# u's normalisation, the modulation and two table loads moved forward within the generation of a convolution kernel, and six reads of u's spectra issued ahead

## Chip, core and metric

One NeuronCore of a Trainium2 chip. The time is device microseconds of one execution. TensorE is called PE, VectorE DVE, ScalarE ACT, GpSimd POOL and SyncE SP, as in the profile.

## What is computed

A layer on 2048 tokens of width 512. A vector c gives six modulation rows of 512. u is normalised, modulated and convolved per channel with a kernel K of 2048 taps that is generated from 128 complex poles; then comes a second modulated block of two mixers.

```python
mod = (_silu(c) @ w_mod).reshape(c.shape[0], 6, 1, -1)        # sa, ca, ga, sb, cb, gb
h = _layernorm(x, axis=-1) * (1 + ca) + sa
# inside _A_ref, on h:
P = jnp.exp(logdA[:, :, None] * l[None, None, :])
K = jnp.einsum("dn,dnl,dn->dl", Cc, P, dB).real
y = irfft(rfft(up, 2 * L) * rfft(Kp, 2 * L))[:L] + u * Dskip
x = x + ga * y
h = _layernorm(x, axis=-1) * (1 + cb) + sb
x = x + gb * _B_ref(h, ...)      # spatial shift mixer (w1, w2), then channel mixer (w3, w4)
```

(The transforms are shown shortened; the reference pads to 2L and uses rfft2.)

## The kernel before

It has three stages in one program. Each engine takes its instructions in the order in which the code issues them (`tc.manual_schedule`), so the order of the source is the order of five queues.

**Generation** (to about 207 us). A loop over k makes the kernel K in 32 chunks. For each chunk PE forms angles (`turns`, L440 to L455: nine pairs of matmuls into a PSUM bank pair `xx`, of which there are two), ACT takes their sine and cosine into a tile `tr` (three of them), DVE multiplies these with magnitudes (`products`, L466, L472 in every second chunk, L475, L476), and PE reduces the products in a burst of 64 small matmuls (`burst`, L498), whose PSUM bank ACT copies to KX after each second chunk. The turns of chunk k + 2 are issued in chunk k, ahead of chunk k's products. The magnitudes of the next four chunks come from `exps`: in chunks 1, 5, 9, ... 25 PE makes five more `xx` banks and ACT takes their exponentials, which needs another function table than the sine, so that a table is loaded ahead of them and another behind.

Other work is hung into the chunks by a list `side[k]`: what it holds is issued at the end of chunk k, and what it puts into `later` at the start of chunk k + 1. The 16 blocks of u are normalised there: `u_stats(i)` (DVE L142, L143, then two small POOL operations), two chunks later `u_norm(i)` (DVE L417, L418), and for each pair of blocks `u_dft` in the two chunks that follow (PE L426), whose results ACT copies to a tile `vs` in `later` and SP stores to the DRAM array VU (L434). `at(i)` gives block i's chunk. The quarters of u (`xu`, two buffers), the six weights of the modulation (`wm`, one buffer; `load_mod`, `mod_parts`, `mod_sum`), and the tables of the second transforms (`load_t2`, L533, into buffers of `xu`; `load_tu`, L537, into that of `wm`) are loaded by SP in the same list.

**Spectra** (to about 305 us). `k_first` (L626) makes eight rounds of K's first transform from KX; ACT copies half of each to VK0 and DVE half to VK1. VK0 lies on memory that generation used, among it that of the `vs` tiles. Then come 16 steps (jh, kc). Step n: PE makes K's spectrum (`spectrum_k`, L680), DVE multiplies it with u's (`multiply`, L690, L692), PE transforms the product of step n - 1 back (`back`, L702), ACT copies that to a tile `z` (two of them), POOL stores z to the DRAM array ZT (L706), PE makes u's spectrum of step n + 1 (`spectrum_u`, L650) from a block read from VU, and ACT copies it to `us`. ACT's order in a step is z, then us. The blocks are read by SP (`load_vu`, L640) into a ring of seven buffers `ld` of 512 KB. The same ring takes w1 (L750) and the blocks of ZT that the inverse reads (L721). The quarters of x (L724), FI and w2 are on SP's queue too. SP waits for nothing but a free buffer and the data's source, so it runs ahead of the loop that issues its loads.

**Mixers** (the rest), bound by PE.

Of the kernel before, what the change touches and what calls it, by code (L numbers as in the profile page):

```python
# [102 lines left out]
def dram(t, off, ap):  # L103
    return bass.AP(tensor=t.tensor, offset=t.offset + off, ap=ap)


def body(ctx, tc, A):
# [100 lines left out]
    def load_mod(n):  # L208
        wmt[n] = KX[:, n * 2048:n * 2048 + 2048].rearrange("p (a b) -> p a b", a=4) if n < 3 else \
            wml.tile([128, 4, 512], F32, name="wm")  # L210
        Y.dma_start(wmt[n].rearrange("p a b -> p (a b)"), A["wm"][MODS[n]])


    def mod_parts(n):
        w = wmt[n]
        m = psu.tile([128, 512], F32, name="pu")
        for i in range(4):
            T.matmul(m[32 * i:32 * i + 32], scb[:, i:i + 1].to_broadcast([128, 32]), w[:, i], start=True, stop=True,
                     skip_group_check=True)
        return lambda: act(w[:, 0], m)  # L220

    def mod_sum(n):
        k = MODS[n]
        m = psu.tile([128, 512], F32, name="pu")
        T.matmul(m, SP4, wmt.pop(n)[:, 0], start=True, stop=True)
        if k in (1, 4):
            return lambda: act(mods[k], m, AF.Identity, bias=1.0)
        return lambda: act(mods[k], m)
# [51 lines left out]
    with tc.manual_schedule():  # L280
# [88 lines left out]
        sg, mc, rc, at, at0 = la.bitcast(I32), tmp("mc"), tmp("rc"), tmp("at"), tmp("at0")  # L369
# [136 lines left out]
    side = {k: [] for k in range(40)}  # L506
    for k in range(8):
        w, i = ("w3", k) if k < 4 else ("w4", k - 4)
        n = A[w].shape[0] // 4
# [1 line left out]
    for k in range(2):  # L511
        side[28 + 3 * k].append(lambda i=k * 256: P.dma_start(WD["w2"][i:i + 256], A["w2"][i:i + 256]))
    for n in range(3, 6):
        k = 7 * n - 9
        side[k - 4].append(lambda n=n: load_mod(n))
        side[k].append(lambda n=n: later.append(mod_parts(n)))
        side[k + 1].append(lambda n=n: later.append(mod_sum(n)))
    at = lambda i: 1 + (i * 28) // 16
    for i in range(16):
        side[max(at(i) - 2, 0)].append(lambda i=i: u_stats(i))  # L520
        side[at(i)].append(lambda i=i: u_norm(i))
# [14 lines left out]
        TU.append(wml.tile([128, 32, 64], F32, name="wm"))  # L536
        Y.dma_start(TU[0], A["TU"].rearrange("p (a b) -> p a b", a=32))  # L537

    side[24].append(load_t2)
    side[29].append(load_tu)  # L540
    side[31].append(load_t2)

    def add_skip(h, g0, g1):
        V.tensor_add(Kq[:, h, g0:g1, 31], DS[:, h * 64 + g0:h * 64 + g1], Kq[:, h, g0:g1, 31])
# [74 lines left out]
    def k_first(r):  # L619
        bank = lambda n: psa.tile([128, 4, 2, 64], F32, name=n)  # L620
        ps = [bank("pk1"), kbank([128, 4, 2, 64]), bank("pz"), kbank([128, 4, 2, 64])]
        kv = KX.rearrange("p (g x) -> p g x", g=64)
        for gl in range(8):
            for j in range(2):
                rows = slice(64 * j, 64 * j + 64)
                T.matmul(ps[2 * j + gl // 4][:, gl % 4].rearrange("p j x -> p (j x)"), kv[rows, r * 8 + gl], FK[rows],  # L626
                         start=True, stop=True)
        for q in (0, 2, 1, 3):
            g0 = r * 8 + q % 2 * 4
            o, i = VK[q // 2][:, :, :, g0:g0 + 4], ps[q].rearrange("p g j x -> p x j g")  # L630
            if q // 2:
                V.tensor_copy(o, i)
            else:
                act(o, i)
# [3 lines left out]
    def load_vu(jh, kc):  # L638
        t = vus[jh, kc] = block()
        Y.dma_start(t, dram(VU, jh * 1048576 + kc * 8 * 16384, [[256, 128], [32768, 4], [1, 256]]))  # L640
# [17 lines left out]
    def flip(kc):  # L658
        t = t3s[kc] = c2.tile([128, 8, 64], F32, name="T3", bufs=3)
        for gh in range(2):  # L660
            r = slice(gh * 64, gh * 64 + 64)
            P.tensor_scalar(t[r], T2[kc // 4][r, kc % 4 * 4:kc % 4 * 4 + 8, 64 - gh * 64:128 - gh * 64], -1.0, None, op0=OP.mult)
# [54 lines left out]
    def load_inv(jh, k, i=None, q=Y):  # L717
        if (jh, k) not in zis:
            zis[jh, k] = block()
        a, n = (0, 4) if i is None else (2 * i, 2)  # L720
        q.dma_start(zis[jh, k][:, a:a + n], dram(ZT[jh], (k * 4 + a) * 32768, [[256, 128], [32768, n], [1, 256]]))  # L721

    def load_x(g):
        Y.dma_start(X2[:, g * 4:g * 4 + 4].rearrange("p b d -> p (b d)"), A["x"][g])  # L724
# [11 lines left out]
    def inverse_parts(jh, g, pl, name):  # L736
        return [inv_half(jh, g, i, pl, name) for i in range(2)]

    def inverse(jh, g):
        for f in inverse_parts(jh, g, psa, "pz"):  # L740
            f()
# [353 lines left out]

    steps = [(jh, kc) for jh in range(2) for kc in range(8)]
    with tc.manual_schedule():
        load_vu(*steps[0])
        flip(0)
        Y.dma_start(Gm, A["G"].rearrange("p (a b) -> p a b", a=2))  # L1100
        for r in range(8):
            k_first(r)
            if r == 3:
                load_vu(*steps[1])
            if r == 6:
                load_vu(*steps[2])
        us = spectrum_u(*steps[0])
        split = None
        for n, st in enumerate(steps):
            p = spectrum_k(*st)  # L1110
            multiply(*st, us, p)
            if n == 7:
                v0x.close()
                pw2 = ctx.enter_context(pool("pw2", side="right", reuse_waits="tile"))
                pw1 = ctx.enter_context(pool("pw1", side="right", reuse_waits="tile"))
                W2h, W2l, ldw2 = weights(pw2, WD["w2"], 512, 512, "w2", 4)
                W1h, W1l, ldw1 = weights(pw1, A["w1"], 512, 512, "w1", 4)
            if n > 0:
                back(*steps[n - 1])
            if n == 15:  # L1120
                i1 = inverse_parts(0, 1, psb, "pk2")
            if n < 15:
                us = spectrum_u(*steps[n + 1])
            if n + 3 < 16:
                load_vu(*steps[n + 3])
            if n % 2 == 0 and n < 14:
                flip(steps[n + 2][1])
            if n in (3, 4, 6, 8):
                load_x(n - 3 if n < 5 else n // 2 - 1)
            if n == 9:  # L1130
                Y.dma_start(FI, A["FI"].rearrange("p (a b c) -> p a b c", a=32, b=2))
            if split:
                split()
                split = None
            if n in (8, 9):
                split = ldw1(two, n % 2 * 2, 2)
            if n == 10:
                for k in (0, 3, 4, 7):
                    load_inv(0, k)
            if n == 12:  # L1140
                inverse(0, 0)
                w2s = [ldw2(None, 2 * i, 2) for i in range(2)]
                for b in range(4):
                    half_stat(b, 0)
            if n == 13:
                inverse(0, 3)
                for k in (1, 2, 5, 6):
                    load_inv(0, k)
            if n in (14, 15):
                w2s.pop()()  # L1150
# [105 lines left out]
        n = cm.tile([128, 2, 512], F32, name="h2")  # L1256
# [18 lines left out]
        r = transposed(n)  # L1275
        split_w(1)
        r = parts_of(r)
# [4 lines left out]
        for g in range(8):  # L1282
            r = chan(g, r)
# [18 lines left out]
```

## Time and profile before

| | us |
|---|---|
| three runs | 688.5, 689.38, 691.06 (median 689.38) |
| profiled execution | 691.26 |
| its span, first to last instruction | 689.5 |
| PE, DVE, ACT, POOL busy | 642.6, 498.0, 331.2, 124.8 |
| mean granted TensorE clock | 0.989 of full |
| waits of POOL for DVE's statistics of u | 140.2 in 15 |
| waits of ACT (z) for stores of ZT | 8.7 in 3 |

The waits of an engine with time to spare cost nothing: POOL has nothing else to do between two statistics. A timeline's row has the start, the duration, the engine, the line, the operation, what is written from what, and in brackets the idle time ahead of it and what ended it. ACT's rows all name L115, the helper through which it is called, so they are told apart by their tiles.

### The profile page before, as it was taken

The page shows a single profiled execution, that of the slowest core. Times are in us where ns is not written, and L with a number is a line of the kernel's source. Part 1 is how long each engine was busy: PE and PEld are TensorE (multiplying, and loading weights), DVE is VectorE, ACT ScalarE, POOL GpSimd, SP SyncE. Part 2 cuts the span into 40 slices and gives each one's busy share as a digit, 9 for nine tenths or more (in the row PEclk, how much of TensorE's full clock was granted, in tenths as well). Part 3 has the DMA queues.
Part 4 walks back from the last instruction along what each step waited for, and adds up shares of the span by engine and source line. Part 5 has one row for each costly group of instructions (what it writes and reads, how often), then busy time and mean ns, then how long its engine had stood idle before and what let it go on. Part 6 is the DMA issues. An engine that isn't in the chain of part 4 may idle for free.

```text
span 689.5 us, 16884 instructions
## 1 busy us (share of the span) xinstructions
PE 642.6 (93%) x7195; PEld 509.2 (74%) x7195; DVE 498.0 (72%) x795; ACT 331.2 (48%) x505; POOL 124.8 (18%) x236
## 2 busy tenths in 40 slices
PE   1899999999999998977998999999999999999996
PEld 0456655655569776634887889999899889898895
DVE  7899999999996887986987967464574536363522
ACT  3878988889875557432444623123131312222121
POOL 4011112112103355413741101001010000000000
PEclk9999999999999999998999999999999999999999
DMA  8603264643739997967387010020100201010001
GB/s 299 284 2 79 75 218 105 209 121 85 275 85 317 354 335 258 346 204 226 108 257 240 1 32 32 16 77 15 47 31 17 77 1 62 1 49 13 1 31 31
DMA packets 51091, 86.42 MB, mean 125 GB/s; under 512 B 4676, under 2 KB 39496, under 8 KB 48424
## 3 DMA queue, kind: packets, MB, share of 16 engines
q1 hardware_dynamic: 46712, 66.74, 30.1%
q0 software_dynamic: 3440, 17.57, 7.4%
q8 instruction: 56, 0.92, 0.6%
q10 hardware_dynamic: 864, 1.05, 0.5%
q14 instruction: 19, 0.16, 0.1%
HBM read 59.12 MB, written 32.90 MB: 133 GB/s over the span
## 4 chain that ended last, share of the span: by engine, by line
PE 70%; DVE 6%; DMA 5%; ACT 3%; POOL 2%; issue 1%; ACTq 0%; SPq 0%; DVEq 0%; POOLq 0%
PE pm L841 7%; PE pm L838 7%; PE pm L839 7%; PE xx L448 7%; PE pa L954 6%; PE pa L955 6%; PE pa L962 6%; PE kp L498 3%; DMA ZT<-z 3%; PE ph L893 2%; PE ph L895 2%; PE ph L892 2%; DMA ld<-ZT 2%; PE pu L426 2%; PE pT L803 2%; PE pk L626 2%
## 5 line engine op out<-in xcount | busy, mean ns | idle before, releaser
L115 ACT ACTIVATE gh<-pm 128x512 fp32r<-128x512 f32 (+1 forms) x48 | 26.9, 560 | 200.7 <-PE pm L841 200.7
L838 PE MATMUL pm<-nh,w3h 128*128 128x256 f32 (+1 forms) x352 | 86.6, 281 | 2.7 <-ACT nh L115 2.7
L839 PE MATMUL pm<-nh,w3l 128*128 128x256 f32 (+1 forms) x352 | 86.3, 280 | 0.1
L946 DVE TENSOR_TENSOR gl<-gf,gh 128x512 fp32r<-128x512 f32 (+1 forms) x48 | 30.8, 643 | 68.4 <-ACT gf L115 68.4
L954 PE MATMUL pa<-w4h,gh 128*128 128x512 f32 (+1 forms) x176 | 69.6, 395 | 0.0
L838 PEld LDWEIGHTS pm<-nh,w3h 128*128 128x128 f32 (+1 forms) x352 | 66.0, 187 | 4.4 <-ACT nh L115 2.9
L955 PE MATMUL pa<-w4l,gh 128*128 128x512 f32 (+1 forms) x176 | 68.9, 392 | 0.0
L839 PEld LDWEIGHTS pm<-nh,w3l 128*128 128x128 f32 (+1 forms) x352 | 65.9, 187 | 2.2 <-DVE w3l L756 0.5
L765 POOL TENSOR_TENSOR rs<-mv,eps_t 128x1 f32<-128x1 f32 (+1 forms) x39 | 11.0, 282 | 282.4 <-DVE mv L771 265.4
L841 PE MATMUL pm<-nl,w3h 128*128 128x256 f32 (+1 forms) x352 | 55.0, 278 | 0.0
L449 PE MATMUL xx<-MG,ON 64*128 64x512 f32 x160 | 48.1, 397 | 0.0
L962 PE MATMUL pa<-w4h,gl 128*128 128x512 f32 (+1 forms) x176 | 48.0, 390 | 0.0
L448 PE MATMUL xx<-MG,ON 64*128 64x512 f32 x160 | 48.0, 396 | 0.0
L841 PEld LDWEIGHTS pm<-nl,w3h 128*128 128x128 f32 (+1 forms) x352 | 47.0, 187 | 0.0
L898 DVE TENSOR_TENSOR h<-h,ph 128x512 f32<-128x512 f32 x16 | 11.0, 687 | 45.1 <-PE ph L895 45.1
L466 DVE SCALAR_TENSOR_TENSOR e<-tr,p 128x512 f32<-128x512 f32 x64 | 41.1, 684 | 1.5 <-ACT tr L115 1.5
L498 PEld LDWEIGHTS kp<-e,e 128*32 128x32 f32 x2048 | 30.1, 110 | 12.7 <-issue 7.6
L475 DVE TENSOR_TENSOR e<-tr,p 128x1024 f32<-128x1024 f32 x32 | 39.0, 1220 | 0.0
L476 DVE TENSOR_TENSOR e<-tr,m 128x1024 f32<-128x1024 f32 x32 | 39.0, 1219 | 0.0
L115 ACT ACTIVATE p<-xx 128x1024 f32<-128x1024 f32 (+1 forms) x40 | 37.5, 979 | 2.2 <-PE xx L252 1.0
L962 PEld LDWEIGHTS pa<-w4h,gl 128*128 128x128 f32 (+1 forms) x176 | 33.0, 188 | 7.3 <-DVE gl L946 0.2
L115 ACT ACTIVATE tr<-xx 128x1024 f32<-128x1024 f32 x32 | 33.0, 1030 | 9.6 <-PE xx L449 7.9
(236 smaller groups left out, 1731.6 us busy)
## 6 DMA issues: line engine op xcount, KB each, us to landing
VU<-vs SPq DMA_DIRECT2D x64, 128.0 KB, 3.7
ld<-VU SPq DMA_DIRECT2D x16, 512.0 KB, 7.4
ZT<-z POOLq DMA_DIRECT2D x30, 256.0 KB, 6.2
ld<-ZT SPq DMA_DIRECT2D x12, 512.0 KB
Dw<-in_w POOLq DMA_DIRECT2D x8, 688.0 KB, 4.7
xu<-in_u SPq DMA_DIRECT2D x4, 1024.0 KB, 8.0
KX<-in_x SPq DMA_DIRECT2D x4, 1024.0 KB, 8.0
GD<-go SPq DMA_DIRECT2D x16, 256.0 KB, 2.3
```

What stands on the lines that cost most here:

```text
L115: return S.activation(out, in_, f, bias=bias, scale=scale)
L448: T.matmul(x[:, :512], la, ma, start=(i == 0), stop=(i == len(ops) - 1))
L449: T.matmul(x[:, 512:], lb, mb, start=(i == 0), stop=(i == len(ops) - 1))
L466: V.scalar_tensor_tensor(e0[:, 1, a], tr[:, 1, 0], 1.0 - 2.0 * a, mg[:, a], op0=OP.mult, op1=OP.mult)
L475: V.tensor_mul(e0[:, 0], tr[:, 0, 0:1].to_broadcast([128, 2, 512]), mg)
L498: T.matmul(kp[32 * j:32 * j + 32, (k % 2) * 4 + g], e1[:, r, d], e0[:, r, :, d * 32:d * 32 + 32], start=(r == 0), stop=(r == 1), skip_grou ...
L838: T.matmul(p, wh[:, k, c], hi[k], start=(k == 0), stop=False)
L839: T.matmul(p, wl[:, k, c], hi[k], start=False, stop=False)
L841: T.matmul(p, wh[:, k, c], lo[k], start=False, stop=(k == 3))
L954: T.matmul(acc[i], gh[:m, e, s], W4h[:m, f], start=(f == 0), stop=False)
L955: T.matmul(acc[i], gh[:m, e, s], W4l[:m, f], start=False, stop=False)
L962: T.matmul(acc[i], gl[:m, e, s], W4h[:m, f], start=False, stop=(f == 10))
```

## The change

Six edits. The blocks of u are spread over 24 chunks instead of 28, so that `at(i)` runs to 23 instead of 27; the quarters of u that are loaded in the list move with it. The modulation's last three parts go from chunks 12, 19 and 26 to 10, 16 and 22. The tables T2, TU, T2 are loaded in chunks 21, 25 and 27 instead of 24, 29 and 31. Six reads of VU are issued ahead of the first rounds, where one was, and the others in the places that a table `ahead` gives. No operation is added or taken away.

```diff
     for n in range(3, 6):
-        k = 7 * n - 9
+        k = 6 * n - 8
         side[k - 4].append(lambda n=n: load_mod(n))
         side[k].append(lambda n=n: later.append(mod_parts(n)))
         side[k + 1].append(lambda n=n: later.append(mod_sum(n)))
-    at = lambda i: 1 + (i * 28) // 16
+    at = lambda i: 1 + (i * 24) // 16
...
-    side[24].append(load_t2)
-    side[29].append(load_tu)
-    side[31].append(load_t2)
+    side[21].append(load_t2)
+    side[25].append(load_tu)
+    side[27].append(load_t2)
...
     with tc.manual_schedule():
-        load_vu(*steps[0])
+        for i in range(6):
+            load_vu(*steps[i])
         flip(0)
         Y.dma_start(Gm, A["G"].rearrange("p (a b) -> p a b", a=2))
         for r in range(8):
             k_first(r)
-            if r == 3:
-                load_vu(*steps[1])
-            if r == 6:
-                load_vu(*steps[2])
         us = spectrum_u(*steps[0])
         split = None
+        ahead = {1: 6, 2: 7, 3: 8, 4: 9, 5: 10, 6: 11, 7: 12, 9: 13, 11: 15}
...
-            if n + 3 < 16:
-                load_vu(*steps[n + 3])
+            if n in ahead:
+                load_vu(*steps[ahead[n]])
...
                 for k in (0, 3, 4, 7):
                     load_inv(0, k)
+                load_vu(*steps[14])
```

The first place is DVE from the end of chunk 25 to the start of chunk 28. e0 and e1 are products, xu is a quarter of u, and p1 and WN are magnitudes and weights of the poles. Before:

```order
L476 TENSOR_TENSOR e1_2572<-tr_2395,m1_2485 128x1024
L417 SCALAR_TENSOR_TENSOR xu_1767<-xu_1767,lum_2451,modu_117 128x512
L418 SCALAR_TENSOR_TENSOR xu_1767<-xu_1767,lur_2454,modu_117 128x512
L142 BN_STATS lus_2639<-xu_1767 128x6
L143 BN_AGGR lum_2640<-lus_2639 128x2
L466 SCALAR_TENSOR_TENSOR e0_2677<-tr_2467,p0_2270 128x512 x2
```

and two chunks on, between chunks 27 and 28:

```order
L476 TENSOR_TENSOR e1_2747<-tr_2546,m1_2681 128x1024
L259 TENSOR_TENSOR p1_2560<-p1_2560,WN_116 128x64x4
L417 SCALAR_TENSOR_TENSOR xu_1767<-xu_1767,lum_2640,modu_117 128x512
L418 SCALAR_TENSOR_TENSOR xu_1767<-xu_1767,lur_2643,modu_117 128x512
L466 SCALAR_TENSOR_TENSOR e0_2814<-tr_2663,p0_2564 128x512 x2
```

The same stretch, chunks 25 to 28, in the changed kernel:

```order
L476 TENSOR_TENSOR e1_2618<-tr_2447,m1_2533 128x1024
L466 SCALAR_TENSOR_TENSOR e0_2716<-tr_2515,p0_2316 128x512 x2
L472 TENSOR_TENSOR m1_2720<-p1_2260 128x1024
L475 TENSOR_TENSOR e0_2716<-tr_2515,p0_2316 128x1024
L476 TENSOR_TENSOR e1_2717<-tr_2515,m1_2720 128x1024
L466 SCALAR_TENSOR_TENSOR e0_2779<-tr_2592,p0_2322 128x512 x2
L475 TENSOR_TENSOR e0_2779<-tr_2592,p0_2322 128x1024
L476 TENSOR_TENSOR e1_2780<-tr_2592,m1_2720 128x1024
L259 TENSOR_TENSOR p1_2606<-p1_2606,WN_116 128x64x4
L466 SCALAR_TENSOR_TENSOR e0_2844<-tr_2702,p0_2610 128x512 x2
```

u's two normalisations and one statistic have left; the products are as they were.

The second place is ACT in the changed kernel from the exponentials of chunk 25 (p0, p1) to the sine and cosine of chunk 28 (tr_2702).

```order
L115 ACTIVATE p0_2668<-xx_2665 128x1024
L115 ACTIVATE p1_2606<-xx_2671 128x768
L115 ACT_TABLE_LOAD
L115 ACTIVATE turn1_357<-hpi_70 128x1
L115 ACTIVATE KX_87<-kp_2537 128x8x64
L115 ACTIVATE vs_2686<-pu_2677 128x512
L115 ACTIVATE vs_2686<-pu_2678 128x512
L115 ACTIVATE tr_2702<-xx_2693 128x1024
L115 ACTIVATE tr_2702<-xx_2704,hpi_70 128x1024
```

Before, the same nine stand at this place, with the results of another pair of u's blocks in vs: nothing moved for ACT here.

The third place is SP's queue behind the last table, which is T2's second half (xu<-in_T2); ld<-VU are the reads of u's spectra, Gm a small table, KX<-in_x a quarter of x. Before:

```order
L533 DMA xu_3042<-in_T2 128x2048
L640 DMA ld_3079<-VU_60 128x4x256
L1100 DMA Gm_3058<-in_G 128x128
L640 DMA ld_3181<-VU_60 128x4x256
L640 DMA ld_3255<-VU_60 128x4x256
L640 DMA ld_3353<-VU_60 128x4x256
L640 DMA ld_3427<-VU_60 128x4x256
L640 DMA ld_3498<-VU_60 128x4x256
L640 DMA ld_3572<-VU_60 128x4x256
L724 DMA KX_87<-in_x 128x2048
L640 DMA ld_3644<-VU_60 128x4x256
L724 DMA KX_87<-in_x 128x2048
```

and in the changed kernel, from the sixth read on:

```order
L640 DMA ld_3089<-VU_60 128x4x256
L1101 DMA Gm_3058<-in_G 128x128
L640 DMA ld_3431<-VU_60 128x4x256
L640 DMA ld_3502<-VU_60 128x4x256
L640 DMA ld_3576<-VU_60 128x4x256
L724 DMA KX_87<-in_x 128x2048
L640 DMA ld_3648<-VU_60 128x4x256
L724 DMA KX_87<-in_x 128x2048
```

Gm moved behind the sixth read, and the first quarter of x from behind the seventh read to behind the ninth; the second quarter from behind the eighth to behind the tenth.

## The prediction

> **What bounds the kernel now.** I read the page first, then the table of stages, then each engine's timeline from 130 to 300 us.
>
> ```profile
> span 689.5 us, 16884 instructions
> ...
> DVE  7899999999996887986987967464574536363522
> ...
> DMA  8603264643739997967387010020100201010001
> ```
>
> A slice is 17.2 us. DVE is full to about 207 us, the generation of the convolution kernel; the DMA engines are full from there to about 260 us, where the spectra are multiplied; from 330 us on PE is full, and the change has no instruction there. The table of stages (PE, PEld, DVE, ACT, POOL busy, clock, DMA share, GB/s) says the same closer:
>
> ```profile
> 170.00:190.00 20.00, 19.52 (x361) 12.49 (x361) 19.74 (x26) 18.00 (x23) 4.45 (x7) 1.00 0.79 262
> 190.00:207.00 17.00, 17.00 (x354) 10.79 (x342) 16.79 (x20) 12.41 (x16) 0.00 (x0) 1.00 0.40 88
> ```
>
> PE looks as full as DVE, but a busy PE is not one at its peak. What decides is the idle time of DVE. Between 36 us and the end of generation its timeline has only these idle spells (in brackets):
>
> ```profile
> 124.51 1.29 DVE L466 SCALAR_TENSOR_TENSOR e<-tr,p 128x512 f32<-128x512 f32 x2 [0.22 <-ACT tr L115]
> ...
> 146.46 1.29 DVE L466 SCALAR_TENSOR_TENSOR e<-tr,p 128x512 f32<-128x512 f32 x2 [0.67 <-ACT tr L115]
> ...
> 190.67 1.29 DVE L466 SCALAR_TENSOR_TENSOR e<-tr,p 128x512 f32<-128x512 f32 x2 [0.21 <-ACT tr L115]
> ...
> 206.85 0.48 DVE L544 TENSOR_TENSOR KX<-DS,KX 128x64 f32<-128x64 f32 x2
> ```
>
> That is 0.22 + 0.67 + 0.21 = 1.1 us in 171. Generation takes as long as DVE's work, so moving that work within it gains at most 1.1 us. But all three spells stand three chunks behind a group of exponentials: ACT had not made the sine in time. ACT is the engine that is nearly late, and u's work on DVE is what covers it.
>
> **Term 1, the end of generation.** The change adds no work there; it moves 16 blocks of u forward, so that DVE's last piece for u is in chunk 23 instead of 27. Here is DVE in chunks 24 to 27 now:
>
> ```profile
> 174.61 1.29 DVE L466 SCALAR_TENSOR_TENSOR e<-tr,p 128x512 f32<-128x512 f32 x2
> ...
> 178.08 0.75 DVE L417 SCALAR_TENSOR_TENSOR xu<-xu,lum,modu 128x512 f32<-128x512 f32 x1
> ...
> 180.44 1.28 DVE L466 SCALAR_TENSOR_TENSOR e<-tr,p 128x512 f32<-128x512 f32 x2
> ...
> 185.04 1.29 DVE L466 SCALAR_TENSOR_TENSOR e<-tr,p 128x512 f32<-128x512 f32 x2
> ...
> 188.51 0.42 DVE L259 TENSOR_TENSOR p<-p,WN 128x256 f32<-128x256 f32 x1
> 188.85 0.75 DVE L417 SCALAR_TENSOR_TENSOR xu<-xu,lum,modu 128x512 f32<-128x512 f32 x1
> ```
>
> The rows of L466 open chunks 25, 26, 27, and that at 190.67 opens 28. The products of 25 take 178.08 - 174.61 = 3.47 us, of 26 185.04 - 180.44 = 4.60, of 27 188.51 - 185.04 = 3.47, L259 0.34: together 11.88. u's work between them takes 180.44 - 178.08 = 2.36 and 190.67 - 0.21 - 188.85 = 1.61, together 3.97, and goes. ACT and PE in the same stretch:
>
> ```profile
> 174.99 1.10 PE L498 MATMUL kp<-e,e 128*32 128x64 f32 x64
> ...
> 178.33 1.03 ACT L115 ACTIVATE tr<-xx 128x1024 f32<-128x1024 f32 x1
> ...
> 180.56 1.28 ACT L115 ACT_TABLE_LOAD   x1
> 181.86 4.90 ACT L115 ACTIVATE p<-xx 128x1024 f32<-128x1024 f32 x5
> 186.77 1.28 ACT L115 ACT_TABLE_LOAD   x1
> ...
> 188.65 1.07 ACT L115 ACTIVATE vs<-pu 128x512 f32<-128x512 f32 x2
> 189.60 1.04 ACT L115 ACTIVATE tr<-xx 128x1024 f32<-128x1024 f32 x1
> ```
>
> The matmuls of chunk 24 (L498) cannot begin before DVE ends that chunk at 174.61. Behind them in PE's order come u's transform, whose eviction ACT makes, and the turns of chunk 27. From 178.33 ACT is never idle until the sine of chunk 28 ends at 190.64: sines, table, five exponentials, table, eviction, sine. None of this goes: in the changed order the transforms of the last blocks stand behind chunks 24 and 25, just where those of the blocks before stood. So from the end of chunk 24 to the start of chunk 28's products this path takes 190.67 - 174.61 = 16.06 us, whatever DVE does, and DVE has 11.88 us left. It will wait **16.06 - 11.88 = 4.2 us** for a sine before chunk 28. The 3.97 us are not saved, since they now stand ahead of chunk 24. The three old spells go, as the earlier groups have as much of u's work behind them as before or more (chunks 17 to 19: two normalisations of about 1.6 and two statistics of about 0.8, against one and one): -1.1. Sum: **+3.1 us** at the end of generation.
>
> Bounds: if the path starts at PE's row, 174.99, and PE has no lag, the wait is 15.68 - 11.88 = 3.8; if the two modulation steps that move from chunks 26 and 27 to 22 and 23 leave PE 1.5 us late there, 5.7; if the old spells stay, 1.1 more; if ACT should run ahead and nothing waits, -1.1. So -1.1 to +5.7, and I take 3.1, since every piece of the path has its own row. Chunks 28 to 31 stay as they are: DVE is never idle there now, and PE and ACT only lose work.
>
> ```profile
> xu<-in_u SPq DMA_DIRECT2D x4, 1024.0 KB, 8.0
> ```
>
> What moves on the queues costs nothing. A quarter of u (8.0 us to land) is asked for four chunks, over 20 us, ahead of its first statistic, as the modulation's tiles are ahead of their matmuls; POOL's roots stay two chunks ahead of the normalisation that reads them; T2 and TU go three or four chunks earlier on SP, among VU's stores, where the DMA share is 0.40 to 0.79. If one of them came late, DVE would wait for it as long as it is late: a whole landing, 8 us, at the worst.
>
> [...]
>
> **Term 2, the step from generation to the spectra.**
>
> ```profile
> 204.72 2.57 SPq L434 DMA_DIRECT2D VU<-vs  x4
> 207.39 0.54 SPq L533 DMA_DIRECT2D xu<-in_T  x1
> 212.65 0.39 SPq L640 DMA_DIRECT2D ld<-VU  x1
> ...
> 220.00 1.67 SPq L724 DMA_DIRECT2D KX<-in_x  x1
> ...
> 212.79 2.56 ACT L115 ACTIVATE VK<-pk 128x512 f32<-128x512 f32 x5 [4.04 <-DMA xu<-in_T]
> ...
> 210.26 1.17 PE L626 MATMUL pk<-FK,KX 64*128 64x128 f32 x17
> ...
> 214.44 1.17 PE L626 MATMUL pk<-FK,KX 64*128 64x128 f32 x17
> ...
> 216.22 1.17 PE L626 MATMUL pk<-FK,KX 64*128 64x128 f32 x17
> ```
>
> ACT's first copy into VK0 waits 4.04 us. The trace names the load of T2; by place, VK0 lies where the eviction buffers vs lay, so it is the last stores of VU, issued up to 207.3. In the changed kernel they end four chunks sooner and the wait goes. But PE's rounds, 216.22 - 214.44 = 1.78 us each, lost only 214.44 - 210.26 - 2 x 1.78 = 0.6 us by it, since the PSUM banks covered the rest: **-0.6**. The 4.04 is not the prize. The first read of VU goes out when the last matmul of generation has freed its buffer, at about 209.3 plus the shift, 3.4 us sooner in its stage; its first reader (224.4) doesn't wait for it now, so that is worth nothing directly.
>
> **Term 3, the spectra.** Six reads ahead are not new: SP runs ahead of the loop, and seven reads are issued between 212.65 and 220.00 now, as many as there are buffers. New is that the first quarter of x (1 MB, L724) stands behind two more reads, of which each needs a buffer that step 0 or 1 must free. It leaves at about 228 instead of 220, and the four quarters each move to about where the next one is now. What waits in this stage:
>
> ```profile
> 245.29 0.69 DVE L690 TENSOR_TENSOR ma<-pk,us 128x512 f32<-128x512 f32 x1 [3.19 <-ACT us L115]
> ...
> 263.19 0.69 DVE L690 TENSOR_TENSOR ma<-pk,us 128x512 f32<-128x512 f32 x1 [2.69 <-ACT us L115]
> ...
> 261.09 1.09 ACT L115 ACTIVATE z<-pz 128x512 f32<-128x512 f32 x2 [4.34 <-DMA ZT<-z]
> ...
> 252.91 8.02 DMA ZT<-z
> ...
> 244.00:248.00 4.00, 4.00 (x76) 2.43 (x78) 2.71 (x5) 3.75 (x9) 2.11 (x4) 1.00 1.07 416
> ```
>
> DVE waits for us, which ACT makes behind z, which waits for a store of ZT two steps old, 8 us long among the reads (the row of the chain at 252.91). The stage is short of DMA, and no byte goes away that is issued in it after 220. One more megabyte now falls between 245 and 262, where the stores are: at 416 GB/s 2.5 us if all of it counts; nothing if it fits into the lulls. Below nothing: 3.19 + 2.69 = 5.9 gained if both waits go. The stores of steps 0 and 1 meet the same reads as before, one of them a quarter of x, so the first wait should stay; of the second, part moves a step or two earlier. I take **+0.7**, near the lower price, as the lulls are short.
>
> [...] The issue rows at 212.65 and 220.00 show the reads as early as their buffers allow already.
>
> **Sum.** 3.1 - 0.6 + 0.7 = +3.2 us. The profiled execution took 691.26 us (span 689.5 and 1.8 around it); it lay 1.9 above the median of the runs, 689.38. So 694.5 beside that execution, and **692.6** beside the median, which I put down. About 0.5%, 3.4 us, is what a measurement of this kernel can tell from no change, and the forecast lies just under it.
>
> **Rivals**, beside the median:
> 1. *DVE is not starved*: PE and ACT get ahead in chunks 20 to 24, so that the exponentials stand ready. For it: PE loses work behind chunk 25. Against: PE's matmuls of chunk 24 need DVE's products, and ACT has no gap. -1.1 - 0.6 + 0.7 = -1.0: 688.4. By this the change doesn't do what its words say for generation, and little else.
> 2. *The change does what the early reads are for*: stores of ZT meet fewer reads and both waits go, with the starved DVE: 3.1 - 0.6 - 5.9 = -3.4: 686.0; together with rival 1, 681.8. Against: the megabyte that comes later.
> 3. *Clearly slower*: x and FI push each other among the stores. It decides once the stores of step 2 land over a microsecond later than now; then the whole megabyte counts (2.5) and PE's lag at chunk 24 too (5.7 - 1.1 = 4.6): 4.6 - 0.6 + 2.5 = +6.5: 695.9.
>
> **How the numbers follow.** Forecast (+2 to +5) 0.55, a little more of it under the bound of 3.4 than over it; rival 1 0.17; rival 2 0.12; rival 3 0.16. Within 0.5%: 0.29 of the forecast, rival 1's 0.17 and 0.03 of rival 2, 0.49. Slower: 0.26 + 0.16 = 0.42. Faster: 0.09. The range reaches from above rival 2's value to a little over rival 3's, 687 to 696.5, and leaves out about 0.15.
>
> **What would show it.** Right: one idle spell of 4 us on DVE's timeline ahead of the first product of chunk 28, put down to ACT's sine, and no other over 0.3; the row of L544 at about 210; no wait of ACT's first VK copy; waits of DVE for us that still add up to about 6. Wrong: L544 at 206 (rival 1), one of the two waits for us gone (rival 2), a new one of over 1 us between 247 and 258 (rival 3). A wait for a normalised block, or for a table, would break the whole account: I price none.

## The result, and the profile after

| | median | runs | profiled execution (span) |
|---|---|---|---|
| before | 689.60 us | 688.50 to 691.06 (4) | 691.26 (689.5) |
| after | 700.51 us | 696.30 to 701.15 (4) | 701.15 (699.4) |

The change makes the kernel **slower: ratio 1.0149, 95% interval 1.0124 to 1.0174**. The forecast was 692.6, with a range to 696.5. The sign of its sum was right, its size was not, and the likeliest of its three outcomes, within 0.5%, was not the one that came.

First the span of the changed kernel, from its page, and the group of the products, from the table of groups by line (behind the bars: busy time, mean ns of one, then the idle time of DVE ahead of them and what ended it). Before, that idle time was `1.5 <-ACT tr L115 1.5`.

```profile
span 699.4 us, 16893 instructions
...
L466 DVE SCALAR_TENSOR_TENSOR e<-tr,p 128x512 f32<-128x512 f32 x64 | 41.1, 684 | 10.6 <-ACT tr L115 9.0 <-PE kp L498 1.6
```

The busy time, 41.1 us, is the same to the digit; only the waiting has grown. DVE's timeline from 36 us to the end of generation says where (in brackets the idle time and what ended it; these are all its idle spells there):

```profile
106.15 1.29 DVE L466 SCALAR_TENSOR_TENSOR e<-tr,p 128x512 f32<-128x512 f32 x2 [0.54 <-ACT tr L115]
112.10 1.29 DVE L466 SCALAR_TENSOR_TENSOR e<-tr,p 128x512 f32<-128x512 f32 x2 [0.43 <-ACT tr L115]
130.89 1.29 DVE L466 SCALAR_TENSOR_TENSOR e<-tr,p 128x512 f32<-128x512 f32 x2 [2.11 <-ACT tr L115]
154.45 1.29 DVE L466 SCALAR_TENSOR_TENSOR e<-tr,p 128x512 f32<-128x512 f32 x2 [0.74 <-ACT tr L115]
182.43 1.29 DVE L466 SCALAR_TENSOR_TENSOR e<-tr,p 128x512 f32<-128x512 f32 x2 [0.57 <-ACT tr L115]
186.77 1.29 DVE L466 SCALAR_TENSOR_TENSOR e<-tr,p 128x512 f32<-128x512 f32 x2 [0.78 <-ACT tr L115]
193.03 1.29 DVE L466 SCALAR_TENSOR_TENSOR e<-tr,p 128x512 f32<-128x512 f32 x2 [1.56 <-PE kp L498]
197.33 0.42 DVE L259 TENSOR_TENSOR p<-p,WN 128x256 f32<-128x256 f32 x1 [0.73 <-ACT p L115]
201.21 1.29 DVE L466 SCALAR_TENSOR_TENSOR e<-tr,p 128x512 f32<-128x512 f32 x2 [3.46 <-ACT tr L115]
217.39 0.48 DVE L544 TENSOR_TENSOR KX<-DS,KX 128x64 f32<-128x64 f32 x2
```

The first four stand ahead of chunks 12, 13, 16 and 20 and add up to 3.82 us. The last five stand ahead of chunks 25, 26 and 27, of the weighting at the end of 27 (L259), and of chunk 28: 7.10. Together 10.92, where there were 1.10. The end of generation (L544) moved from 206.85 to 217.39, by 10.54; the waits are 9.82 of it.

Two more rows close the account, the first matmul of the spectra (L650) and the first normalisation behind the inverse (L774):

```profile
234.30 1.09 PE L650 MATMUL pk<-ld,wm 64*64 64x256 f32 x16
328.27 1.36 DVE L774 SCALAR_TENSOR_TENSOR h<-KX,mv,modg 128x512 f32<-128x512 f32 x2
```

In the kernel before they are:

```profile
224.36 1.09 PE L650 MATMUL pk<-ld,wm 64*64 64x256 f32 x16
317.91 1.36 DVE L774 SCALAR_TENSOR_TENSOR h<-KX,mv,modg 128x512 f32<-128x512 f32 x2
```

L650 is 9.94 later, so the step from generation to the spectra gained 0.60. L774 is 10.36 later, so the spectra lost 0.42. The span is 9.9 longer, so the mixers gave back 0.46. In this pair of executions all of the loss is in generation.

One thing there was not in the forecast at all: TensorE's granted clock (the third column from the end in the table of stages, whose columns are as in the prediction).

```profile
93.00:104.00 11.00, 11.00 (x79) 5.82 (x69) 10.78 (x15) 7.64 (x11) 1.97 (x3) 0.53 0.20 66
```

In the kernel before, such a stretch is shorter:

```profile
97.00:101.00 4.00, 4.00 (x31) 2.75 (x35) 4.00 (x6) 3.60 (x6) 0.00 (x0) 0.57 0.58 232
```

Inside the first stretch, from 94 to 103 us, the clock is 0.50: half of full. A mean of 0.53 over 11 us is then 2 x 0.47 x 11 = 10.3 us at half clock; 0.57 over 4 us is 3.4. The waits ahead of chunks 12 to 20 come behind the one, the three old spells (124, 146, 191 us) behind the other.

### The profile page after: what moved, and what is told of

Same layout as the page of the kernel before. It is cut to its first block, busy times and chain, and to the rows that moved or that the text cites. A ratio compares the mean times of both kernels' runs of the same rounds, so it can differ in the third digit from the quotient of the medians.

```text
span 699.4 us, 16893 instructions
## 1 busy us (share of the span) xinstructions
PE 648.0 (93%) x7195; PEld 511.1 (73%) x7195; DVE 498.6 (71%) x795; ACT 332.4 (48%) x505; POOL 122.7 (18%) x236
## 4 chain that ended last, share of the span: by engine, by line
PE 53%; DVE 7%; DMA 6%; issue 2%; POOL 2%; ACT 1%; ACTq 0%; DVEq 0%; POOLq 0%
PE pm L841 7%; PE pm L839 7%; PE pm L838 7%; PE pa L962 6%; PE pa L954 6%; PE pa L955 6%; DMA ZT<-z 4%; PE ph L893 2%; PE ph L895 2%; PE ph L892 2%; PE pk L626 2%; DMA ld<-ZT 2%; PE pT L803 2%; PE pk L680 1%; PE pz L702 1%
## 5 line engine op out<-in xcount | busy, mean ns | idle before, releaser
L115 ACT ACTIVATE gh<-pm 128x512 fp32r<-128x512 f32 (+1 forms) x48 | 26.9, 560 | 200.6 <-PE pm L841 200.6
L466 DVE SCALAR_TENSOR_TENSOR e<-tr,p 128x512 f32<-128x512 f32 x64 | 41.1, 684 | 10.6 <-ACT tr L115 9.0
L115 ACT ACTIVATE p<-xx 128x1024 f32<-128x1024 f32 (+1 forms) x40 | 37.6, 980 | 5.1 <-PE xx L252 3.5
L680 PE MATMUL pk<-VK,xu 64*64 64x128 f32 x768 | 38.7, 272 | 0.1
```

What stands on the lines that cost most here:

```text
L115: return S.activation(out, in_, f, bias=bias, scale=scale)
L466: V.scalar_tensor_tensor(e0[:, 1, a], tr[:, 1, 0], 1.0 - 2.0 * a, mg[:, a], op0=OP.mult, op1=OP.mult)
L680: T.matmul(p[gh][kk * 64:kk * 64 + 64, i, ro], w, VK[jh][rows, ri * 32 + k1].rearrange("p j g -> p (j g)"), start=(ri == 0), stop=(ri == 1 ...
```

## Experiments

Two theories stood against each other. **Cover**: DVE waits because u's work no longer stands behind the last group of exponentials (chunk 25), and because PE is late there by its own work. **Clock**: the loss is the longer stretch at half clock. A third, that the reads cost the time, was kept as a check. The table has each kernel against the kernel before on the same chip, and from its one profiled execution the start of L544 and the sum of DVE's waits from 36 us to there.

| kernel | ratio to before (95%) | L544 | DVE's waits | L544 less waits |
|---|---|---|---|---|
| before | | 206.85 | 1.10 | 205.75 |
| the change | 1.0149 (1.0124 to 1.0174) | 217.39 | 10.92 | 206.47 |
| gen | 1.0156 (1.0103 to 1.0209) | 213.46 | 7.46 | 206.00 |
| reads | 1.0022 (1.0005 to 1.0038) | 205.41 | 0 | 205.41 |
| mod | 1.0148 (1.0125 to 1.0172) | 217.39 | 11.51 | 205.88 |
| uonly | 1.0146 (1.0121 to 1.0172) | 214.04 | 8.27 | 205.77 |
| tail | 1.0082 (1.0054 to 1.0109) | 210.12 | 4.42 | 205.70 |
| spread20 | 1.0172 (1.0148 to 1.0196) | 216.17 | 9.92 | 206.25 |
| modfree | 1.0052 (1.0031 to 1.0073) | 211.41 | 5.52 | 205.89 |
| nofill | 1.0272 (1.0248 to 1.0296) | 221.83 | 15.71 | 206.12 |
| mod26 | 1.0113 (1.0073 to 1.0152) | 211.03 | 5.22 | 205.81 |
| morefill | 1.0160 (1.0137 to 1.0184) | 215.49 | 9.52 | 205.97 |
| bfill | 1.0042 (1.0023 to 1.0060) | 208.10 | 2.26 | 205.84 |
| keep28 | 0.9973 (0.9955 to 0.9992) | 205.51 | 0 | 205.51 |

The last column is the first finding: in fourteen kernels it stays between 205.4 and 206.5. DVE's own work in generation is nearly the same in all of them, so its waits are what differs, and each wait can be priced by its row.

### The parts of the change alone

**gen** has the generation of the change (all three edits there) and the reads of before; its edit is the first two hunks of the diff.

> The edits of generation alone (u's blocks over 24 chunks, the modulation at 6n-8, the tables at 21, 25, 27); the reads of the spectra as before. Cover theory (DVE waits because u's work no longer stands where ACT's groups of exponentials need cover, and PE is late by the denser work): the end of generation (first row of L544) at 216 to 218 instead of 206.9, the whole time +9 to +11, so 699 to 701. Clock theory (the time goes by how long TensorE is held at half clock, about 10 us near 95 us in the profiled execution of the change against 3.5 before): only the 4 to 6 us of waits from chunk 24 on stay if the held stretch is 3 to 4 us here, so L544 at 211 to 213 and the whole at 693 to 696; 5 us more only if the held stretch is again about 10 us. Reads theory (the loss comes from the reads after all): within 2 us of before.

Measured: 700.09 us, as slow as the whole change. Its profiled execution was its fastest, 696.12. Its waits, from DVE's timeline:

```profile
150.52 1.29 DVE L466 SCALAR_TENSOR_TENSOR e<-tr,p 128x512 f32<-128x512 f32 x2 [0.37 <-ACT tr L115]
178.50 1.30 DVE L466 SCALAR_TENSOR_TENSOR e<-tr,p 128x512 f32<-128x512 f32 x2 [0.56 <-ACT tr L115]
182.85 1.29 DVE L466 SCALAR_TENSOR_TENSOR e<-tr,p 128x512 f32<-128x512 f32 x2 [0.78 <-ACT tr L115]
189.11 1.29 DVE L466 SCALAR_TENSOR_TENSOR e<-tr,p 128x512 f32<-128x512 f32 x2 [1.56 <-PE kp L498]
193.40 0.43 DVE L259 TENSOR_TENSOR p<-p,WN 128x256 f32<-128x256 f32 x1 [0.73 <-ACT p L115]
197.28 1.29 DVE L466 SCALAR_TENSOR_TENSOR e<-tr,p 128x512 f32<-128x512 f32 x2 [3.46 <-ACT tr L115]
```

The generation is the same program as in the change, instruction for instruction. The last five waits are the same to 0.01 us (7.09 against 7.10). Before chunk 25 there is 0.37 instead of 3.82, and this execution has no half clock near 95 us, only 3.4 us of it near 55 (and 3.4 more from 211 us on, at the very end). So the account has two parts: **about 7.1 us that the order makes, and a part that comes with half clock.** The other three runs of gen took 697.62, 702.57 and 703.79 at mean granted clocks of 0.986, 0.978 and 0.975, against 0.989 for the profiled one. Neither theory alone had this; the cover theory gave too much for the order, the clock theory too little.

**reads** is the kernel before with the other three hunks only.

> The six reads ahead alone, generation as before. Cover theory and clock theory alike: L544 at 206 to 208; ACT's first copy into VK0 still waits about 4 us for the last stores of VU; from step 0 to the inverse's first normalisation (L774) 0 to +1 us longer; the whole within 1 us of before. Reads theory: +3 or more.

Measured: 690.82, 0.22% slower, which both theories had. From 36 us on DVE has no wait in this generation, which is that of the kernel before, and TensorE no half clock in it: the three old spells, 1.1 us, come with the half clock near 97 us of the execution that was profiled. ACT's wait for the last stores stays, as forecast:

```profile
211.45 2.56 ACT L115 ACTIVATE VK<-pk 128x512 f32<-128x512 f32 x5 [4.14 <-DMA VU<-vs]
```

**mod** moves the modulation alone, **uonly** u's blocks alone (one line each, the rest as before).

```diff
-        k = 7 * n - 9
+        k = 6 * n - 8
```

> The modulation's steps alone at chunks 10, 16, 22 instead of 12, 19, 26; u's blocks, tables and reads as before. Cover theory: u's work still stands behind every group of exponentials, so DVE's waits grow by 0 to 1.5 us, at chunks 25 and 26 (PE late by the modulation in chunk 22) and perhaps at 16; L544 at 207 to 208.5. Clock theory: the same unless the held stretch near 95 us is longer than 3.5 us, then half of the excess on top.

```diff
-    at = lambda i: 1 + (i * 28) // 16
+    at = lambda i: 1 + (i * 24) // 16
```

> u's blocks alone over 24 chunks; modulation at chunks 12, 19, 26, tables and reads as before. Cover theory: a wait of 4 to 6 us ahead of chunks 27 and 28, more if the modulation's step at 26 and 27 adds to PE there, and 1 to 4 us elsewhere; L544 at 212 to 217, the whole +5 to +10. Clock theory: L544 at 211 to 212 with a held stretch of 3 to 4 us, and 5 more with one of 10 us. If the loss belongs to the modulation's move, L544 at 210 or below.

Measured: 699.59 and 699.51, each as slow as both together. For mod every theory was wrong, by 9 us. uonly came near the cover theory: L544 at 214.04 as expected, 0.67 + 0.73 + 3.46 = 4.86 us of waits at chunks 27 and 28, and the whole 0.5 us above its range. PE's timeline shows what was overlooked; here is uonly, whose wait of 3.12 us ahead of chunk 16 follows:

```profile
122.21 1.02 PE L225 MATMUL pu<-wm,sp 128*128 128x512 f32 x2
123.16 1.07 PE L426 MATMUL pu<-xu,FU 64*64 64x512 f32 x2
125.90 1.08 PE L426 MATMUL pu<-xu,FU 64*64 64x512 f32 x6 [1.67 <-ACT modg L115]
```

u's transform (L426) takes two PSUM banks of the pool `pu`, the sum of a modulation step (L225) one, and the pool has two. Where both fall in one chunk, PE stands here until ACT has evicted the sum (1.67 us in the last row); and in a chunk with exponentials ACT is busy with these (before, 4.90 us for five of them and 1.28 for each table, in the rows of the prediction). In uonly, whose generation is at full clock throughout, it is chunk 13. In mod it is chunk 17, where the wait is 1.67 again and DVE then waits 6.33 ahead of chunk 20 (155.27 us), with 3.4 us of half clock in between; two more such stretches stand near 54 and 123 us in that execution, so not all of mod's 11.51 us is the bank's. The sums of the change lie in chunks 11, 17 and 23 and its transforms in 3, 4, 6, 7, ... 24, 25: no sum meets one. (The first part of a step, L218, takes a bank too, in chunks 10, 16 and 22, and there it does meet one; what that did is told further down.) So the two edits need each other, and what one alone costs says little about the pair.

**modfree** tests that: the modulation earlier too, but with its sums in chunks 9, 16 and 23, which no transform of the kernel before uses.

```diff
-        k = 7 * n - 9
+        k = 7 * n - 13
```

> The kernel before with the modulation's steps at chunks 8, 15 and 22, so that the sum of a step (chunks 9, 16, 23) never falls into a chunk in which u's transform takes both of its PSUM banks; the modulation alone at 10, 16, 22 had sums at 11 and 17, where it does, and was 10.6 us slower. Bank theory (PE stands still until ACT, busy with a group of exponentials, evicts the sum): no wait of PE for modg, no wait of DVE over 1 us, L544 at 205 to 208, the whole within 3 us of before. Density theory (any modulation step earlier than 12, 19, 26 makes PE late): +6 or more, as it was with 10, 16, 22.

Measured: 693.17, 6.4 us better than mod, with no wait of PE for modg. That is as the bank theory has it, but the two profiled executions differ in the clock too (three stretches at half clock in mod's generation, none in modfree's), so how much of the 6.4 us is the bank's is not shown. And some loss stays: DVE waits 2.85 ahead of chunk 20 and 0.73 + 1.94 at chunk 28. The steps now stand at 15 and 22, ahead of the groups in chunks 17 and 25; before, they stood at 19 and 26, behind them.

### The cover

**tail** keeps the last four blocks of u where they were before.

```diff
-    at = lambda i: 1 + (i * 24) // 16
+    at = lambda i: 1 + (i * (24 if i < 12 else 28)) // 16
...
-    side[27].append(load_t2)
+    side[31].append(load_t2)
```

> The changed kernel, but the last four blocks of u are normalised at chunks 22, 23, 25 and 27 as before (their transforms follow, the second half of T2 is loaded at 31); the first twelve blocks, the modulation and the reads stay as changed. Cover theory (DVE waits because nothing of u is left behind the group of exponentials in chunk 25): DVE's waits ahead of chunks 25 to 28, 7.1 us in the changed kernel, fall to 0 to 1.5; L544 at 207 to 210, the whole 689 to 694. Clock theory (the loss is from stretches at half clock in the denser first 24 chunks): no more than 2 us better than the changed kernel, 698 to 701.

Measured: 695.02. DVE's waits:

```profile
150.04 1.29 DVE L466 SCALAR_TENSOR_TENSOR e<-tr,p 128x512 f32<-128x512 f32 x2 [2.98 <-ACT tr L115]
193.94 1.29 DVE L466 SCALAR_TENSOR_TENSOR e<-tr,p 128x512 f32<-128x512 f32 x2 [1.44 <-ACT tr L115]
```

The wait of 7.1 us ahead of chunks 25 to 28 falls to 1.44, as the cover theory has it. Not all of the 5.66 is cover: with no transform of u in chunks 21 and 22, PE's burst of chunk 24 also comes only 1.60 us behind DVE (178.25 and 176.65), where the change has 3.69. By that estimate about 3.6 are left for the cover, near the 3.97 us of DVE's work that stands there again. The whole is 1 us above its range, for a reason that is the theory's own: with twelve blocks early and four late, no block is normalised between chunks 17 and 22, and the group in chunk 17 has lost its cover. There a wait of 2.98 came up (chunk 20).

**spread20** packs u's blocks closer still.

```diff
-    at = lambda i: 1 + (i * 24) // 16
+    at = lambda i: 1 + (i * 20) // 16
```

> The changed kernel with u's blocks over 20 chunks instead of 24, everything else the same. Cover theory: the group of exponentials in chunk 21 loses its cover too, so a second wait of about 4 us stands ahead of chunk 24, beside the one of 3.5 to 4.2 ahead of chunk 28; L544 at 219 to 222, the whole 702 to 706. Clock theory, or a loss from the modulation's place: no new wait at chunk 24, the whole within 3 us of the changed kernel.

Measured: 701.62, L544 3 us earlier than expected, but with the second wait just where the cover theory puts it, ahead of chunk 24 (179.45), beside that ahead of chunk 28 (199.99):

```profile
171.27 1.29 DVE L466 SCALAR_TENSOR_TENSOR e<-tr,p 128x512 f32<-128x512 f32 x2 [1.57 <-PE kp L498]
175.56 0.42 DVE L259 TENSOR_TENSOR p<-p,WN 128x256 f32<-128x256 f32 x1 [0.73 <-ACT p L115]
179.45 1.29 DVE L466 SCALAR_TENSOR_TENSOR e<-tr,p 128x512 f32<-128x512 f32 x2 [3.46 <-ACT tr L115]
192.78 1.29 DVE L466 SCALAR_TENSOR_TENSOR e<-tr,p 128x512 f32<-128x512 f32 x2 [0.54 <-PE kp L498]
197.08 0.43 DVE L259 TENSOR_TENSOR p<-p,WN 128x256 f32<-128x256 f32 x1 [0.73 <-ACT p L115]
199.99 1.29 DVE L466 SCALAR_TENSOR_TENSOR e<-tr,p 128x512 f32<-128x512 f32 x2 [2.49 <-ACT tr L115]
```

The last of them is smaller (2.49 instead of 3.46); no transform of u is left for PE and ACT beside the group in chunk 25, which would explain it. The early waits are nearly gone (0.40 in all), though u's work is denser: density alone doesn't make them.

**mod26** puts the last modulation step back behind the group.

```diff
-        k = 6 * n - 8
+        k = (10, 16, 26)[n - 3]
...
-    side[25].append(load_tu)
+    side[29].append(load_tu)
```

> The changed kernel with its last modulation step at chunks 26 and 27, as before, instead of 22 and 23 (and the table that takes over its buffer loaded at 29, as before); the other two steps at 10 and 16, u's blocks and the reads as changed. Cover theory: 22 and 23 lie ahead of the group of exponentials in chunk 25, so the step's eight and two matmuls (1.04 + 1.12 us) make the whole chain up to chunk 28 late; at 26 and 27 they come behind the turns of chunk 28. DVE's waits ahead of chunks 25 to 28 fall from 7.1 to 4.8 to 5.6 us, L544 by about 2, the whole 694 to 698. If the step's place doesn't matter: 6.8 to 7.4 us there.

Measured: 697.67 (693.78 to 702.05). The waits at the end are 0.67 + 0.73 + 3.46 = 4.86:

```profile
186.66 1.29 DVE L466 SCALAR_TENSOR_TENSOR e<-tr,p 128x512 f32<-128x512 f32 x2 [0.67 <-PE kp L498]
190.96 0.43 DVE L259 TENSOR_TENSOR p<-p,WN 128x256 f32<-128x256 f32 x1 [0.73 <-ACT p L115]
194.85 1.29 DVE L466 SCALAR_TENSOR_TENSOR e<-tr,p 128x512 f32<-128x512 f32 x2 [3.46 <-ACT tr L115]
```

In these executions the place of this step is worth 7.10 - 4.86 = 2.24 us, about PE's time for its matmuls (1.04 + 1.12).

### The clock

**nofill** leaves out the five matmuls that only keep PE busy beside each group of exponentials.

```diff
-                    fill(3)
...
-                        if u < 4:
-                            fill(1)
```

> The changed kernel without the five matmuls of no use beside each group of exponentials (L482; 5 x 0.22 us of PE's work in each of seven groups). Clock theory: TensorE falls to half clock behind more of the groups, each such stretch of 3.4 us or more costing up to 1.7 us, so generation ends 3 to 10 us later than in the changed kernel and the mean clock falls below 0.985. Cover theory with PE late by its own work: the waits ahead of chunks 25 to 27 (2.9 us) shrink by 1 to 2 us if no stretch at half clock comes near them; the wait of 3.5 us ahead of chunk 28 shrinks by no more than 1.

Measured: 708.83, 8.3 above the change, at mean clocks of 0.959 to 0.963. In the profiled execution 4.4 of it lie in generation (L544); the rest comes behind it, where the edit has no instruction, and 2.2 of that in the spectra, which have 3.4 us at half clock from 299 us on. The table of stages has a stretch at half clock behind each of the seven groups:

```profile
53.00:57.00 4.00, 3.69 (x18) 2.68 (x19) 3.97 (x7) 3.97 (x6) 1.45 (x2) 0.57 0.00 0
74.00:81.00 7.00, 6.82 (x58) 4.36 (x62) 6.87 (x10) 5.95 (x8) 1.98 (x3) 0.52 0.41 151
97.00:102.00 5.00, 4.80 (x22) 2.14 (x24) 4.88 (x7) 4.79 (x7) 0.00 (x0) 0.66 0.02 3
121.00:129.00 8.00, 7.49 (x28) 3.67 (x30) 6.18 (x11) 7.49 (x11) 2.71 (x5) 0.57 0.27 63
149.00:153.00 4.00, 4.00 (x15) 2.08 (x15) 3.89 (x7) 3.87 (x6) 1.47 (x3) 0.57 0.55 176
169.00:177.00 8.00, 7.22 (x29) 3.62 (x30) 7.89 (x10) 7.39 (x11) 1.16 (x3) 0.57 0.89 308
196.00:204.00 8.00, 7.81 (x30) 4.07 (x32) 3.54 (x5) 7.40 (x10) 0.00 (x0) 0.57 0.28 111
```

So a group is the lull in which the clock falls here, and those matmuls mostly prevent it: by the same reckoning as above the seven stretches add up to about 37.6 us at half clock, where the change has 10.3 in its generation. Less work on PE did not help: L544 came 4.4 us later, so in generation the clock cost more than the work.

**morefill** doubles them in chunks 1, 5 and 9 of the change; **bfill** does so in the kernel before.

```diff
-                    fill(3)
+                    fill(3 if k > 9 else 6)
...
-                            fill(1)
+                            fill(1 if k > 9 else 2)
```

> The changed kernel with twice the matmuls of no use (6, 2, 2 instead of 3, 1, 1) beside the groups of exponentials in chunks 1, 5 and 9, where DVE is the late one. Clock theory (with them gone TensorE fell to half clock behind all seven groups; with u's denser work they no longer suffice in some executions): no stretch at half clock from 40 to 110 us, no wait of DVE over 0.6 us before chunk 20, times closer together, the whole 695 to 698. If those stretches cost nothing, or the added 1.1 us of PE's work in each group counts instead: 700 to 704.

> The same doubling of the matmuls of no use in chunks 1, 5 and 9, in the kernel before. Clock theory: the stretch at half clock near 97 us and the three waits of DVE behind it (1.1 us) go where they occur, 0 to 1.5 us faster. If the added work counts: 1 to 3 us slower.

Measured: 700.90 and 691.63. In morefill's profiled execution TensorE is at full clock from 36 to 213 us, and the waits up to chunk 20 are still 1.57 + 0.77 (chunks 16 and 20); bfill is 0.42% slower. The expectation of the clock theory fell in both. In bfill generation is at full clock, and the three old spells stand where they stood (0.69, 0.68 and 0.18 ahead of chunks 16, 20 and 28), with two new ones. So they need PE to be late, and not half clock as such: three groups with about 1.2 us more of PE's work (in morefill the rows of L482 in such a group are 1.67, 0.73 and 0.73 us long, against 0.96, 0.50 and 0.50 in mod26) gave 2.26 us of waits, one stretch of 3.4 us at half clock gave 1.10 in the kernel before, and neither gave none (reads). PE has no slack to give here; PE and DVE are both nearly the bound.

**keep28** is aimed at something that the profiles showed beside the change: about 7 us at half clock (3.4 in mod26) behind a gap in which PE waits for reads of ZT, in the kernel before from 312 us on.

```diff
-        keep(6)
+        keep(28)
```

> The kernel before with 28 instead of 6 matmuls of no use (L1165) in the gap of 6.45 us at 307 us, where PE waits for reads of ZT; nothing else. TensorE runs at half clock for 7 us behind that gap in each execution seen. If it is the gap that causes it: no half clock between 310 and 320 us, and 1 to 3 us faster, as L731 there takes 4.09 us for 32 matmuls against 1.93 at full clock and DVE waits for it. If PE isn't what is waited for: within 0.7 us.

Measured: 687.93, ratio 0.9973 (0.9955 to 0.9992), **a little faster than the kernel before**, and so than both. PE's matmuls behind the gap, in keep28:

```profile
304.76 6.65 PE L1165 MATMUL pT<-w1h 128*128 128x512 f32 x28
312.46 2.59 PE L731 MATMUL py<-ld,FI 128*32 128x256 f32 x32 [1.06 <-DMA ld<-ZT]
316.27 1.93 PE L731 MATMUL pm<-ld,FI 128*32 128x256 f32 x32 [1.22 <-DMA ld<-ZT]
```

Before, the two L731 rows took 4.09 and 3.09 us. The granted clock from 310 to 320 us is 1.00 instead of 0.66.

## Why the prediction was wrong, and where it was right

**Term 1, forecast +3.1, measured +10.5.** The length of the path itself was read rightly. From the burst of chunk 24 on PE to the products of chunk 28 on DVE the forecast had 190.67 - 174.99 = 15.68 us. After the change:

```profile
185.55 1.10 PE L498 MATMUL kp<-e,e 128*32 128x64 f32 x64
```

201.21 - 185.55 = 15.66, and in gen and tail 15.66 and 15.69. The wait at chunk 28 came out as 0.73 + 3.46 = 4.19, against 4.2.

That it is 4.2 again is luck: ahead of chunk 27 DVE is held until PE's burst of chunk 25 is done (1.56 us, 193.03), and from there the same 0.73 + 3.46 follow in gen, uonly and mod26, whatever went before.

*The step that failed* is "So from the end of chunk 24 to the start of chunk 28's products this path takes 190.67 - 174.61 = 16.06 us, whatever DVE does". It took 201.21 - 181.86 = 19.35. The path was let begin when DVE ends chunk 24, because PE's burst came right behind it before (174.61 and 174.99, 0.38 later). That was a coincidence. The burst starts 0.32 us behind the matmul ahead of it on PE (174.67), as the bursts of chunks 22 and 23 do (0.33 and 0.31), so DVE did not hold it up; and that of chunk 23 comes 4.3 us behind the end of DVE's chunk 23 (167.32):

```profile
171.66 1.10 PE L498 MATMUL kp<-e,e 128*32 128x64 f32 x64
```

So the path begins where PE's own work has got to. In the change DVE ends chunk 24 at 182.43 - 0.57 = 181.86, but PE's burst comes at 185.55, **3.69 us later**. The bound for this was 1.5. With it, the forecast's own formula gives 15.66 + 3.69 - 11.88 = 7.47, where 7.10 was measured.

What makes PE late is the modulation step in chunks 22 and 23, together with u's transforms in 21 and 22. With both, the burst is 3.69 behind DVE; with the step but without these transforms 1.60 (tail); with the transforms but without the step 0.60. Here is mod26, the start of chunk 25 on DVE and the burst of chunk 24 on PE:

```profile
177.82 1.29 DVE L466 SCALAR_TENSOR_TENSOR e<-tr,p 128x512 f32<-128x512 f32 x2
178.42 1.10 PE L498 MATMUL kp<-e,e 128*32 128x64 f32 x64
```

The step was named as a risk and mis-sized. Beside its own matmuls (1.04 + 1.12) its first part holds one of the two banks of `pu`, so that u's transform in chunk 22 takes 2.3 us (176.64 to 178.93) instead of 1.0 (186.58 to 187.60 in chunk 24):

```profile
177.92 1.08 PE L426 MATMUL pu<-xu,FU 64*64 64x512 f32 x6 [0.21 <-ACT wm L115]
```

That mod26 still waits 4.86, and not 4.19, goes with a path that is longer there, 194.85 - 178.42 = 16.43 us instead of 15.66; why it is longer stays open.

*The second failed step* is "The three old spells go, as the earlier groups have as much of u's work behind them as before or more", priced at -1.1. They were put down to missing cover, three chunks behind a group. reads and keep28 have the same generation, no half clock in it, and no wait: in the execution that was profiled the spells came with the clock, and bfill shows that what they need is a late PE. In the change, waits of this kind were 3.82 us in the profiled execution with 10.3 us at half clock, and 0.37 in gen's with 3.4. The rows of the table of stages that the forecast rested on begin at 170 us, where the clock is 1.00; the stretch at 97 us had no part in it. Over the four runs of the change the time goes with the mean clock too (696.30 at 0.991, 700.48 to 701.15 at 0.987 to 0.989).

**Term 2, forecast -0.6, measured -0.60.** ACT's first copy into VK0 no longer waits for the stores, only 1.84 us for PE, and PE gains what was forecast and not the 4.04 of the row. That it is the same to the hundredth is partly luck: five kernels in which ACT still waits there take 17.2 to 18.4 us from L544 to L650, six in which it doesn't 16.9, and three more that are at half clock near the end of generation 18.0 to 18.1. (mod and tail are among the six, though their last blocks of u stand where they stood: the wait can go without the earlier stores.)

```profile
221.13 0.60 ACT L115 ACTIVATE VK<-pk 128x512 f32<-128x512 f32 x1 [1.84 <-PE pz L626]
```

**Term 3, forecast +0.7, measured +0.42 in this pair, about +1.4 over all runs.** The first quarter of x left behind the ninth read, at 238.65 us, and DVE's waits for us still add up to 3.27 + 1.19 + 0.62 + 0.52 = 5.6, in more and smaller pieces, as forecast:

```profile
238.65 0.54 SPq L724 DMA_DIRECT2D KX<-in_x  x1
...
255.32 0.69 DVE L690 TENSOR_TENSOR ma<-pk,us 128x512 f32<-128x512 f32 x1 [3.27 <-ACT us L115]
268.12 0.69 DVE L690 TENSOR_TENSOR ma<-pk,us 128x512 f32<-128x512 f32 x1 [1.19 <-ACT us L115]
```

With reads alone the whole was 0.22% slower, 1.5 us; the early reads bring nothing. Single executions differ more than the term itself, but the profiles together agree with that: L650 to L774 takes 93.5 to 96.2 us in the seven kernels with the early reads (median 94.4) and 91.7 to 93.6 in the six that read as before (median 93.0; keep28 is left out, as its edit lies there). So the term is about +1.4, twice the forecast.

**Queue moves, forecast nothing:** right. No wait for a table, a quarter of u or a normalised block appears.

**Rivals.** The third, clearly slower at 695.9, came nearest. Its condition came half true: counted from L650, the first two stores of step 2 land 1.2 us sooner than before and the last two 1.9 and 2.5 us later (274.34 and 275.38), and the new wait of 1.19 us at 268.12 is near its sign; the price was 0.4 to 1.4 and not 2.5. What it had right, PE late at chunk 24, is the part that should have been the forecast. Rival 1 held that PE and ACT get ahead; they fall behind.

**What stays open** is why executions of the changed generation fall to a lower mean clock (gen 0.975 to 0.989, mod26 0.982 to 0.992) than those of the kernel before beside them (0.985 to 0.994). Their profiles show the stretches, not their cause.

## What to carry to other kernels

Where two engines are both nearly full, work that "only moves" on one of them is cover for the other: ask at each later lull what stands there afterwards, and also when the engine that feeds the path arrives there, since a path that kept its length to 0.02 us started 3.3 us later. A side job belongs behind a group that is nearly late, not ahead of it (2.24 us for the last modulation step, mod26 against the change). And count the banks of a shared pool chunk by chunk before two schedules are shifted against each other.

## What the hardware showed that I had not expected

TensorE falls to half clock in the middle of stages in which it is never idle for long, and for multiples of one length: 2 x (1 - clock) x window gives 3.4 us (53 to 57, 97 to 102 and 149 to 153 us in nofill), 6.7 to 6.9 (its other four), 3.4 before and 10.3 after. Added up from windows of 1 us, the stretch from 312 to 320 us in the kernel before has 6.82 and that from 93 to 104 us in the change 10.24, two and three times 3.41. In the 3.41 us ahead of the seven falls in nofill PE is busy for 2.35 to 2.54 us by the profile, ahead of the fall in the change for 2.44, and in the kernel before for 3.07; in none of these three executions is it idle for more than about 0.6 us at a time from 36 to 205 us (0.47 before, 0.60 in the change). How full is full enough, no run here shows: reads and keep28 pass the place where the kernel before fell without falling. What sets the length, no run shows either.

22 matmuls of no use in a gap behind the spectra were worth 0.27% of this kernel, and fifteen more beside three of the groups in generation cost 0.42%: the same remedy paid where PE would have been idle for 6.45 us, and cost where it is nearly the bound (busy for 19.52 of the 20 us from 170 us on in the kernel before).
